# Where the low half of a split weight is subtracted: VectorE, or a summing transfer issued by GpSimd

## The chip, the cores and the metric

The kernel runs on one core of one Trainium2 chip. The metric is device time in microseconds (us) of one execution. TensorE is called PE, VectorE DVE, ScalarE ACT, GpSimd POOL and SyncE SP, as in the profile.

## The reference

```python
def _attn_ref(q, k, v):                      # q, k, v: (8, 8, 576, 64)
    scores = (1.0 / np.sqrt(D)) * np.matmul(q, k.transpose(0, 1, 3, 2))
    mask = (rel >= 0) & (rel < 64)           # rel: query position less key position
    scores = np.where(mask, scores, -1000000000.0)
    attn = np.exp(scores - np.max(scores, axis=-1, keepdims=True))
    attn = attn / (np.sum(attn, axis=-1, keepdims=True) + 1e-09)
    return np.matmul(attn, v)

def _moe_ref(x, w_in, w_out):                # x: (4608, 512), w_in: (512, 2048), w_out: (2048, 512)
    h = x @ w_in
    g = h * np.tanh(np.log1p(np.exp(h)))     # Mish
    return g @ w_out
```

Attention in a sliding window of 64 keys is followed by a feed-forward layer with Mish. The inputs and the output are float32.

## The kernel before, in words

**Split numbers.** Float32 products are made of three products of rounded numbers (type fp32r). Every operand is split into a high part, which is its value rounded to fp32r, and a low part, which is the value less the high part; then high times high, high times low and low times high are summed. For the activations these are `xh`, `xl`, `gh`, `gl`; for the weights `wi_h`, `wi_l`, `wo_h`, `wo_l`, which stay in SBUF for the whole run.

**Weight pieces.** The weights arrive in 32 pieces of 128 x 512 elements, 16 of `w_in` and 16 of `w_out`, in alternation. They are called here by kind and number in the order of work: in0, in1, out0, in2, out1, in3, out2, in4 and so on. The weights come as 64-bit words (512 KB for a piece), and DVE makes float32 of them: `w_abs` takes the sign off (on DVE, or on ACT as an Abs activation while the attention of the start runs), and `w_bits` has four steps, called [0] to [3] here, of which [0] and [1] are a TENSOR_SCALAR and [2] and [3] a SCALAR_TENSOR_TENSOR. The finished float32 piece stands in a tile `wa` (`af` in the code). Then `w_round` lets ACT copy it into the fp32r tile of the high part (a CAST in the profile), and `w_rest` lets DVE subtract the high part from `wa` into the low part.

**Buffers.** `wa` shares the pool tag "t" (4 buffers) with `t`, the float32 Mish result, and with the output tile `o`. So an instruction that begins a new tile of this tag waits until the last reader of an older one is done.

**Stages.** The tokens are worked in 12 chunks of 384. In the **prelude** the attention of chunks 0 and 1 runs in eight units (four pairs of heads for each chunk, u = 0 to 7, and a closing round u = 8). A unit is: score products on PE; mask and row maximum on DVE; six exponentials on ACT; sum, reciprocal on DVE; the normalising product on POOL (`pr<-pr,sm`); transposes on PE into `t_ps`; two copies `pT<-t_ps`, one on ACT and one on DVE; value products on PE (`o_ps`); and the split of the result into `xh` (ACT) and `xl` (DVE). A generator, `stream`, deals the weight work into the units: `OPS` says how many of its steps a unit takes (three or four), and `w_round` stands at the end of each unit.

After it come the **steps**, one for each chunk and each 128 of the 2048 hidden columns: twelve products `h_ps`, two Mish activations on ACT (`t` and `gh`, from the same bank), the residue `gl` = `t` - `gh`, and nine products `acc`. There are two `h_ps` banks, so the products of a step need the Mish activations of two steps earlier. Chunks 0 and 1 go through the steps together, in the order (0,0), (0,1), (0,2), (1,0), (0,3), (1,1) and so on, written (chunk, column block). In these first 32 steps the function `weights` works about one piece for each step, and `gl` is made on DVE. After that POOL makes `gl`, and the attention of later chunks is spread between the steps.

**What sets the order.** In the prelude and the first 32 steps the instructions of DVE, ACT, POOL and SP stand in the order in which the code issues them (`InTurn`); later ones are ordered by a scheduler. Each engine works its instructions strictly one after the other. Between the last unit and the steps, POOL builds the masks of the later chunks (`build_masks`), which takes memsets, affine selects and copies.

Of the kernel before, what the change touches and what calls it, by code (L numbers as in the profile page):

```python
# [10 lines left out]
F32 = mybir.dt.float32  # L11
# [4 lines left out]
ALU = mybir.AluOpType  # L16
# [13 lines left out]
def tile_window_attn_mish_ffn(  # L30
# [11 lines left out]
    NPAIR, _, NT = qT.shape  # L42
    NF, _, NC_, _ = w_in.shape
# [73 lines left out]
    vec, act, pool, load = (InTurn(e) for e in (nc.vector, nc.scalar, nc.gpsimd, nc.sync))  # L117
# [263 lines left out]
    loaded, worked, rounded = [], [], []  # L381

    def w_load():
        if pieces:
            fn, f = pieces.pop(0)
            loaded.append(fn(f))

    def w_abs(by_act):

        if not loaded:  # L390
            return
        st, wh, wl, first = loaded.pop(0)
        words = st.bitcast(U32).rearrange("p (n two) -> p n two", two=2)
        lo, hi = words[:, :, 0], words[:, :, 1]
        a = mp.tile([P, WP], U32, name="wa", tag="t", bufs=4)
        af = a.bitcast(F32)
        if by_act:
            act.activation(af, hi.bitcast(F32), AF.Abs)
        else:
            vec.tensor_scalar(a, hi, 0x7FFFFFFF, None, ALU.bitwise_and)  # L400
        worked.append([lo, hi, a, af, wh, wl, 0])

    def w_bits(parts=range(4)):

        for part in parts:
            at = next((i for i, w in enumerate(worked) if w[-1] == part), None)
            if at is None:
                continue
            lo, hi, a, af, wh, wl, _ = worked[at]
            worked[at][-1] += 1  # L410
            if part == 0:
                vec.tensor_scalar(af, af, BIG, TINY, ALU.min, ALU.max)
            elif part == 1:
                vec.tensor_scalar(a, a, 3, 0x3FFFFFFF, ALU.logical_shift_left, ALU.bitwise_and)
            elif part == 2:
                vec.scalar_tensor_tensor(a, hi, 0xC0000000, a, ALU.bitwise_and, ALU.bitwise_or)
            else:
                vec.scalar_tensor_tensor(a, lo, 29, a, ALU.logical_shift_right, ALU.bitwise_or)
                rounded.append([af, wh, wl, False])
                worked.pop(at)  # L420

    def w_round():
        for r in rounded:
            if not r[3]:
                act.copy(r[1], r[0])
                r[3] = True

    def w_rest():
        while rounded and rounded[0][3]:
            af, wh, wl, _ = rounded.pop(0)  # L430
            vec.tensor_tensor(wl, af, wh.bitcast(F32), ALU.subtract)


    slow = []
# [190 lines left out]
    def stream():  # L625

        while True:
            w_bits([0])
            yield
            if rounded and rounded[0][3]:  # L630
                w_rest()
                yield
            w_bits([1])
            yield
            w_bits([2])
            w_abs(True)
            yield
            w_bits([3])
            w_load()
            yield  # L640
# [3 lines left out]
    early = []  # L644
    products_of(0)
    ops = stream()
    for u in range(U + 1):
        now = u < U
# [40 lines left out]
        if u == U:  # L689
            rest_high(u - 1)  # L690
            rest_low(u - 1)
        w_round()
        if now:
            a.te_transpose(p, [at_bank("t_ps") if u == U - 1 else acc_bank(h, "t_ps") if u == U - 2 else h_bank("t_ps") for h in range(2)])

    w_rest()
    while not worked or worked[0][-1] != 2 or len(worked) > 1:
        if not worked:
            w_abs(False)
        w_bits([worked[0][-1]])  # L700
        if not worked:
            w_load()
            w_round()
# [16 lines left out]
    def weights():  # L720
        residue()
        w_abs(False)
        w_bits([2])
        w_rest()
        w_bits([0, 3, 1])
        w_load()
# [26 lines left out]
    for n, (c, f) in enumerate(steps):  # L753
# [14 lines left out]
        if held[0]:  # L768
            w_round()
            if n not in SCORES:  # L770
                weights()
            if last - 3 <= n < last - 1:
                third.load(n - last + 3, "v")
            if last < n < last + NPAIR:
                third.values(n - last - 1, h_bank)
# [47 lines left out]
```

## Time and profile before

| | |
|---|---|
| median of 3 runs (lowest to highest) | 920.12 us (919.44 to 920.77) |
| the profiled execution | 919.01 us, of which the span is 917.2 us |
| granted TensorE clock, mean | 0.999 |
| PE busy | 893.5 us, 97% of the span |
| ACT busy | 388.3 us, 42% |
| DVE busy | 280.1 us, 31% |
| POOL busy | 184.1 us, 20% |

The rows of a timeline give start, length, engine, line of the code, operation, output and inputs, and in brackets how long the engine sat idle before and what ended that. Line 111 is the helper through which most instructions of DVE, ACT, POOL and SP are issued, and line 120 the one for matmuls, so the tile names tell the groups apart. A group's row gives the busy time, the mean length of one in ns, and the idle time ahead of it.

### The profile page before, as it was taken

What the parts mean: (1) busy time and instruction counts of PE and PEld (TensorE: products, weight loads), DVE (VectorE), ACT (ScalarE), POOL (GpSimd) and SP (SyncE); (2) the same over time, 40 slices, a digit from 0 to 9 for tenths busy, and PEclk for the clock granted to TensorE, in tenths of its full rate; (3) what the DMA queues carried; (4) which work ended last, traced back from release to release, by engine and by line L of the source; (5) the groups of instructions that cost most, each with busy time, mean ns of one, the idle gap of its engine ahead of it and who ended that gap; (6) DMA issues with size and microseconds to landing.
All of it is one profiled execution on the core that took longest, in us unless ns stands there. A gap on an engine that the chain in (4) does not pass through costs nothing.

```text
span 917.2 us, 18683 instructions
## 1 busy us (share of the span) xinstructions
PE 893.5 (97%) x7344; PEld 801.2 (87%) x7344; DVE 280.1 (31%) x1054; ACT 388.3 (42%) x1108; POOL 184.1 (20%) x202
## 2 busy tenths in 40 slices
PE   4799999999999999999999999999999999999998
PEld 3588889888898998998999999999999898899996
DVE  5998898213213032032130230321312303200000
ACT  5843654346545255244342442543524515422211
POOL 3310000021222221222222122122222222122221
PEclk9999999999999999999999999999999999999999
DMA  7834352422322033123121321321213203210000
GB/s 242 267 121 148 123 190 82 136 79 79 102 91 78 21 111 96 27 87 100 46 80 55 95 76 60 91 81 62 84 33 115 78 23 100 69 27 1 35 0 35
DMA packets 84951, 78.56 MB, mean 86 GB/s; under 512 B 11136, under 2 KB 76160, under 8 KB 84864
## 3 DMA queue, kind: packets, MB, share of 16 engines
q1 hardware_dynamic: 79680, 67.94, 24.3%
q10 hardware_dynamic: 5184, 9.44, 2.8%
q8 instruction: 58, 0.95, 0.4%
q14 instruction: 29, 0.24, 0.1%
HBM read 56.10 MB, written 9.44 MB: 71 GB/s over the span
## 4 chain that ended last, share of the span: by engine, by line
PE 94%; ACT 2%; SPq 1%; DVE 1%; DMA 1%; issue 0%; ACTq 0%
PE acc L120 44%; PE h_ps L120 43%; PE o_ps L120 4%; PE s_ps L120 3%; SPq L111 1%; ACT pr L111 1%; DMA k_t<-kT 1%; DVE pT L111 0%; ACT xh L111 0%; DMA pT<-tr 0%; DVE pr L111 0%; DVE wa L111 0%; DVE sm L111 0%; ACT L111 0%; DVE wo_l L111 0%
## 5 line engine op out<-in xcount | busy, mean ns | idle before, releaser
L111 ACT ACTIVATE t<-h_ps 128x384 f32<-128x384 f32 x192 | 94.5, 492 | 449.3 <-PE h_ps L120 427.0
L111 POOL TENSOR_TENSOR gl<-t,gh 128x384 fp32r<-128x384 f32 x160 | 162.1, 1013 | 588.8 <-ACT gh L111 587.3
L120 PE MATMUL h_ps<-xh,wi_h 128*128 128x384 f32 x768 | 259.2, 338 | 0.0
L120 PE MATMUL h_ps<-xh,wi_l 128*128 128x384 f32 x768 | 259.2, 337 | 0.0
L120 PE MATMUL h_ps<-xl,wi_h 128*128 128x384 f32 x768 | 257.9, 336 | 0.0
L120 PE MATMUL acc<-wo_h,gh 128*128 128x512 f32 x576 | 228.8, 397 | 0.0
L120 PE MATMUL acc<-wo_l,gh 128*128 128x512 f32 x576 | 226.8, 394 | 0.0
L120 PE MATMUL acc<-wo_h,gl 128*128 128x512 f32 x576 | 223.5, 389 | 0.0
L120 PEld LDWEIGHTS h_ps<-xh,wi_h 128*128 128x128 f32 x768 | 144.2, 188 | 8.6
L120 PEld LDWEIGHTS h_ps<-xl,wi_h 128*128 128x128 f32 x768 | 144.2, 188 | 7.1
L120 PEld LDWEIGHTS h_ps<-xh,wi_l 128*128 128x128 f32 x768 | 144.0, 188 | 0.0
L120 PEld LDWEIGHTS acc<-wo_h,gl 128*128 128x128 f32 x576 | 108.1, 188 | 24.3
L120 PEld LDWEIGHTS acc<-wo_h,gh 128*128 128x128 f32 x576 | 108.0, 187 | 20.4
L120 PEld LDWEIGHTS acc<-wo_l,gh 128*128 128x128 f32 x576 | 108.3, 188 | 14.8
L111 ACT ACTIVATE pr<-pr,mx 128x96 f32<-128x96 f32 (+1 forms) x288 | 105.2, 367 | 9.0 <-DVE mx L111 8.8
L283 DVE CAST xh<-o_ps 128x256 fp32r<-128x256 f32 x16 | 6.8, 425 | 332.9 <-PE o_ps L120 332.9
L111 ACT ACTIVATE gh<-h_ps 128x384 fp32r<-128x384 f32 x192 | 93.2, 485 | 0.0
L111 DVE CUSTOM_DVE_ANT_0 pr<-s_ps,mask 128x96 f32<-128x96 f32 (+1 forms) x288 | 55.2, 258 | 32.4 <-PE s_ps L120 27.3
L363 DVE COPY o<-acc 128x512 f32<-128x512 f32 x12 | 8.3, 691 | 171.6 <-PE acc L120 171.6
L111 ACT ACT_TABLE_LOAD x45 | 57.7, 1283 | 5.5 <-DVE mx L111 4.8
L111 ACT ACTIVATION_READ_ACCUMULATOR pr<-pr,mx 128x1 f32 x288 | 53.9, 187 | 0.0
L120 PEld LDWEIGHTS o_ps<-pT,v_t 128*64 128x64 f32 x1152 | 38.1, 139 | 16.6 <-ACT pT L111 6.5
(45 smaller groups left out, 463.7 us busy)
## 6 DMA issues: line engine op xcount, KB each, us to landing
v_t<-vN SPq DMA_DIRECT2D x48, 384.0 KB, 4.3
pT<-tr SPq DMA_DIRECT2D x480, 24.0 KB, 1.8
k_t<-kT SPq DMA_DIRECT2D x47, 224.0 KB, 5.0
out<-o ACTq DMA_DIRECT2D x36, 256.0 KB, 2.5
q_t<-qT SPq DMA_DIRECT2D x47, 192.0 KB, 4.5
st<-w_in SPq DMA_DIRECT2D x16, 512.0 KB, 3.6
st<-w_out SPq DMA_DIRECT2D x16, 512.0 KB, 3.5
q_t<-qT SPq DMA_DIRECT2D x3, 64.0 KB, 2.1
```

The costliest lines, as they stand in the source:

```text
L111: i = call(*args, **kw)
L120: order.append(nc.tensor.matmul(*args, **kw).ins)
L283: nc.vector.tensor_copy(xh[:, :cut], o_ps[0])
L363: nc.vector.tensor_copy(o, acc[t])
```

## The change

`w_rest` does nothing any more. `w_round` takes each finished piece, copies it on ACT into the high part as before, lets ACT write the negated value (rounded to fp32r, so the negated high part) into the low part, and lets POOL issue a transfer that adds `wa` to the low part in place. The step of `stream` that was the subtraction is gone from the generator, so with the same `OPS` its other steps move up.

```diff
     def w_round():
-        for r in rounded:
-            if not r[3]:
-                act.copy(r[1], r[0])
-                r[3] = True
+        while rounded:
+            af, wh, wl, _ = rounded.pop(0)
+            act.copy(wh, af)
+            act.mul(wl, af, -1.0)
+            pool.dma_start(wl, af, accum_op=ALU.add)
 
     def w_rest():
-        while rounded and rounded[0][3]:
-            af, wh, wl, _ = rounded.pop(0)
-            vec.tensor_tensor(wl, af, wh.bitcast(F32), ALU.subtract)
+        pass
...
         while True:
             w_bits([0])
             yield
-            if rounded and rounded[0][3]:
-                w_rest()
-                yield
             w_bits([1])
```

Three places of the new order follow. In brackets stands what a row waits for: an engine's name, `DMAHW` for a transfer that SP or ACT issues, and `DMASW` for one that POOL issues. Eight `DMASW` semaphores are used in turn, so DMASW0 to DMASW7 are the transfers of in0, in1, out0, in2, out1, in3, out2 and in4, and the next pieces begin with DMASW0 again.

ACT at the end of the prelude, before, from the first Mish to the third:

```order
L111 ACT_TABLE_LOAD
L111 ACTIVATE t<-h_ps 128x384 [waits Activation_49]
L111 ACTIVATE gh<-h_ps 128x384
L111 CAST wo_h<-wa 128x512 [waits DVE_49]
L111 CAST xh_577<-o_ps 128x384 [waits PE_49]
L111 COPY pT_107<-t_ps 128x3x4x32 [waits PE_49,Activation_49]
L111 ACTIVATE t<-h_ps 128x384 [waits DVE_49,Activation_49]
L111 ACTIVATE gh<-h_ps 128x384
L111 CAST xh_577<-o_ps 128x384 [waits PE_49]
L111 CAST wi_h<-wa 128x512
L111 CAST wo_h<-wa 128x512 [waits DVE_49]
L111 ACTIVATE t<-h_ps 128x384 [waits PE_49,Activation_49]
```

ACT at the same place now, from the first Mish to the second (the Abs of a weight piece is the row `wa<-st`):

```order
L111 ACT_TABLE_LOAD
L111 ACTIVATE t<-h_ps 128x384 [waits DMASW3_49]
L111 ACTIVATE gh<-h_ps 128x384
L111 CAST wi_h<-wa 128x512 [waits DVE_49]
L111 ACTIVATE wi_l<-wa 128x512
L111 CAST xh_587<-o_ps 128x384 [waits PE_49]
L111 ACT_TABLE_LOAD [waits DMAHW6_49,DMASW4_49]
L111 ACTIVATE wa<-st 128x512 [waits Activation_49]
L111 COPY pT_107<-t_ps 128x3x4x32 [waits PE_49]
L111 ACT_TABLE_LOAD [waits DMASW5_49]
L111 ACTIVATE t<-h_ps 128x384 [waits Activation_49]
L111 ACTIVATE gh<-h_ps 128x384
```

The piece cast behind the first Mish is in3 and no longer out1, an Abs has come between the two Mish steps with a table load on each side, and the second Mish stands behind a wait for the transfer of in3.

ACT in the rows that follow now, up to the fourth Mish:

```order
L111 CAST xh_587<-o_ps 128x384 [waits PE_49]
L111 CAST wo_h<-wa 128x512 [waits DVE_49]
L111 ACTIVATE wo_l<-wa 128x512
L111 CAST wi_h<-wa 128x512 [waits DVE_49]
L111 ACTIVATE wi_l<-wa 128x512
L111 ACTIVATE t<-h_ps 128x384 [waits DMASW6_49,PE_49,Activation_49]
L111 ACTIVATE gh<-h_ps 128x384
L111 CAST wo_h<-wa 128x512 [waits DVE_49]
L111 ACTIVATE wo_l<-wa 128x512
L111 ACTIVATE t<-h_ps 128x384 [waits DMASW7_49,PE_49,Activation_49]
```

The third Mish waits for the transfer of out2 and the fourth for that of in4, where the third waited before for PE and ACT alone.

POOL between the last normalising product and the steps, now (before, the masks follow the product at once and no transfer stands here):

```order
L111 DMA wi_l<-wa 128x512 [waits Activation_49]
L111 DMA wo_l<-wa 128x512 [waits DVE_49,Activation_49]
L111 MEMSET mask 128x128
L111 AFFINE_SELECT mask<-mask 32x96 [waits Pool_49]
L111 AFFINE_SELECT mask<-mask 32x96 x3
L111 AFFINE_SELECT mask<-mask 32x96 [waits Pool_49] x4
L111 COPY mask_83<-mask 128x128 [waits Pool_49]
L111 MEMSET mask_83 32x64 [waits Pool_49]
L111 MEMSET mask_83 32x32
L111 COPY mask_84<-mask 128x128 [waits Pool_49]
...
L111 DMA wi_l<-wa 128x512 [waits DVE_49,Activation_49]
```

The transfers of in3 and out2 stand ahead of the masks and that of in4 behind them.

## The prediction

> **What bounds the kernel now.** I read the page of the profile first, for the busy shares and the chain that ended last:
>
> ```profile
> span 917.2 us, 18683 instructions
> PE 893.5 (97%) x7344; PEld 801.2 (87%) x7344; DVE 280.1 (31%) x1054; ACT 388.3 (42%) x1108; POOL 184.1 (20%) x202
> PE 94%; ACT 2%; SPq 1%; DVE 1%; DMA 1%; issue 0%; ACTq 0%
> ```
>
> PE carries the run; it is idle for 917.2 - 893.5 = 23.7 us in all. The windows by stage say where (columns: length, then busy time and count of PE, PE's weight loads, DVE, ACT and POOL, then clock, share of the DMA engines, GB/s):
>
> ```profile
> 0.00:23.00 23.00, 11.43 (x152) 8.52 (x154) 12.41 (x63) 12.26 (x46) 7.93 (x20) 1.00 0.75 242
> 23.00:46.00 23.00, 16.83 (x273) 13.55 (x268) 21.64 (x94) 20.63 (x79) 8.31 (x8) 1.00 0.87 265
> 46.00:69.00 23.00, 21.98 (x135) 20.02 (x134) 21.39 (x46) 10.08 (x21) 3.90 (x14) 1.00 0.38 124
> 69.00:92.00 23.00, 23.00 (x160) 20.60 (x159) 18.56 (x50) 7.50 (x17) 0.00 (x0) 1.00 0.44 147
> ```
>
> Nearly all of it, 11.6 + 6.2 + 1.0 us, lies ahead of 69 us. From there PE is full although DVE, which makes the weights, is busy 18.6 of 23 us. So a lighter DVE buys nothing behind the prelude; the change can gain only what it takes off the prelude, and it loses whatever it makes PE wait. The timeline of PE shows where the prelude ends:
>
> ```profile
> 47.59 0.82 PE L301 MATMUL t_ps<-ident,pr 128*128 128x128 f32 x6
> 48.70 0.33 PE L120 MATMUL o_ps<-pT,v_t 128*64 128x64 f32 x2 [0.30 <-ACT pT L111]
> 49.75 0.91 PE L120 MATMUL o_ps<-pT,v_t 128*64 128x64 f32 x22 [0.72 <-DVE pT L111]
> 50.59 0.44 PE L120 MATMUL h_ps<-xh,wi_h 128*128 128x384 f32 x1
> ...
> 54.84 0.33 PE L120 MATMUL h_ps<-xh,wi_h 128*128 128x384 f32 x1
> ...
> 63.17 0.33 PE L120 MATMUL h_ps<-xh,wi_h 128*128 128x384 f32 x1
> ```
>
> The last wait is at 49.75, for DVE's copy of the last unit's `pT`. The products of step (0,2) start at 50.59, of (1,0) at 54.84 and of (1,1) at 63.17; two steps take 63.17 - 54.84 = 8.33 us, without a gap.
>
> **The change part by part: what goes and what comes.** The groups by form give the prices:
>
> ```profile
> L111 DVE TENSOR_TENSOR wo_l<-wa,wo_h 128x512 fp32r<-128x512 f32 x16 | 11.0, 688 | 0.2 <-ACT wo_h L111 0.2
> L111 DVE TENSOR_TENSOR wi_l<-wa,wi_h 128x512 fp32r<-128x512 f32 x16 | 11.0, 686 | 0.1
> L111 ACT CAST wi_h<-wa 128x512 fp32r<-128x512 f32 x16 | 9.9, 621 | 10.4 <-DVE wa L111 10.4
> L111 ACT ACT_TABLE_LOAD x45 | 57.7, 1283 | 5.5 <-DVE mx L111 4.8
> L111 POOL TENSOR_TENSOR gl<-t,gh 128x384 fp32r<-128x384 f32 x160 | 162.1, 1013 | 588.8 <-ACT gh L111 587.3
> L111 DVE TENSOR_SCALAR wa<-wa 128x512 uint32<-128x512 uint32 x32 | 13.5, 422 | 0.1
> ```
>
> DVE loses 32 subtractions, 22.0 us. ACT gains 32 negations; the nearest row is the cast over the same tile, 0.62 us (0.51 from start to start, as the rows below show). ACT also gains two table loads of 1.28 us at the end of the prelude, because the stream, one step shorter, now brings an Abs between the first two Mish steps. POOL gains 32 issues and the DMA engines 32 transfers of 128 x 512 float32, 256 KB each. From 69 us on ACT has 15 idle us in 23 and PE needs none of this soon, so there I cost the negations and transfers at nothing.
>
> **The units of the prelude.** The waits ahead of an exponential show ACT's room:
>
> ```profile
> 31.11 0.40 ACT L111 ACTIVATE pr<-pr,mx 128x128 f32<-128x128 f32 x1 [0.42 <-DVE mx L111]
> ...
> 40.22 0.40 ACT L111 ACTIVATE pr<-pr,mx 128x128 f32<-128x128 f32 x1 [0.82 <-DVE mx L111]
> ```
>
> A unit is a loop: exponentials, then on DVE the sum, one weight step, reciprocal, the copy of `pT` and the next masks. The subtractions of DVE stood mostly beside the exponentials, off this loop; the negations fill the 0.42 to 0.82 us that ACT waits. Walking the new order through with the row lengths of before, units 3 and 6 start up to 0.5 us earlier or later, and the eighth unit's exponentials start at 40.2, as before. I cost the units at nothing, with 1 us either way.
>
> **The end of the prelude: +1.05 us.** Timelines of ACT and of DVE:
>
> ```profile
> 44.16 1.28 ACT L111 ACT_TABLE_LOAD   x1
> 45.46 0.49 ACT L111 ACTIVATE t<-h_ps 128x384 f32<-128x384 f32 x1
> 45.85 0.48 ACT L111 ACTIVATE gh<-h_ps 128x384 fp32r<-128x384 f32 x1
> 46.22 0.62 ACT L111 CAST wo_h<-wa 128x512 fp32r<-128x512 f32 x1
> 46.73 0.49 ACT L111 CAST xh<-o_ps 128x384 fp32r<-128x384 f32 x1
> 48.17 0.48 ACT L111 COPY pT<-t_ps 128x384 f32<-128x384 f32 x1 [0.95 <-PE t_ps L301]
> 48.92 0.49 ACT L111 ACTIVATE t<-h_ps 128x384 f32<-128x384 f32 x1 [0.27 <-DVE wo_l L111]
> ```
>
> ```profile
> 47.25 0.56 DVE L111 TENSOR_TENSOR xl<-o_ps,xh 128x384 fp32r<-128x384 f32 x1 [1.13 <-ACT xh L111]
> 47.73 0.43 DVE L111 TENSOR_SCALAR wa<-wa 128x512 f32<-128x512 f32 x1
> 48.08 0.74 DVE L111 TENSOR_TENSOR wo_l<-wa,wo_h 128x512 fp32r<-128x512 f32 x1
> ...
> 49.15 0.54 DVE L111 COPY pT<-t_ps 128x384 f32<-128x384 f32 x1
> ```
>
> Now, from the cast at 46.22: negation 46.73 to 47.30, `xh` at 47.24, table load 47.6 to 48.9, Abs to 49.5, ACT's `pT` to 49.95 (before 48.65). DVE stands behind that Abs with step [0], at 49.5, then step [1] at 49.85 and its `pT` copy at 50.2, where before it came at 49.15. So the value products end their wait at 50.8 for 49.75, and every later product of PE is 1.05 us late.
>
> **The wait chain in the first steps: +2.3 us.** Let L be the time from the end of a negation until its transfer is reported done. A Mish begins a new tile of tag "t" and now waits for transfers. Second Mish: in3's transfer is done at 47.3 + L, a table load follows, so it starts at 48.6 + L. With the spacing of the rows above (Mish to `gh` 0.39, `gh` to the next 0.37, 0.37 for `xh`, 0.51 for a cast), the negation of out2 ends at 50.8 + L. Third Mish: out2's transfer, 50.8 + 2L. On POOL the issue of out2 (taken as 1.0 us by the nearest row, 1013 ns for a product over such a tile; between 0.4 and 1.5 it matters little) is followed by the masks:
>
> ```profile
> 45.52 0.21 POOL L111 MEMSET mask<- 128x128 f32 x1
> ...
> 49.80 0.52 POOL L111 COPY mask<-mask 128x128 f32<-128x128 f32 x1
> ```
>
> They take 50.32 - 45.52 = 4.8 us, and nobody waited for that before. Now in4's transfer queues behind them: issue at 50.8 + L + 1.0 + 4.8 = 56.6 + L, done at 56.6 + 2L, and the fourth Mish with its `gh` has left its bank 0.9 later, at 57.5 + 2L. The products of (1,1) need that bank at 63.17 + 1.05 = 64.2. PE therefore waits 2L - 6.7 us if that is above nothing. The third Mish asks for less (2L + 51.7 against 60.05), and later Mish steps catch up as long as 1.9 us of ACT work and L fit into the 8.33 us of two steps.
>
> L is not in this trace: no transfer here is issued by POOL or sums. The nearest rows, issue to landing:
>
> ```profile
> v_t<-vN SPq DMA_DIRECT2D x48, 384.0 KB, 4.3
> pT<-tr SPq DMA_DIRECT2D x480, 24.0 KB, 1.8
> k_t<-kT SPq DMA_DIRECT2D x47, 224.0 KB, 5.0
> ```
>
> The low end is the small transfer from SBUF to SBUF plus 256 KB at 320 GB/s (0.98 of the engines moved 314 GB/s in a row quoted below), 1.8 + 0.8 = 2.6 us; the high end is the 224 KB row with 1.0 for the issue and as much again for reading the destination, 7.0. I take 4.5, by the two rows nearest in size, 4.3 and 5.0. The wait is then 2 x 4.5 - 6.7 = 2.3 us. By the Trainium skill (DMA: Bandwidth & Descriptors, section "Anatomy of one DMA — SWDGE (gpsimd) path") a transfer issued by GpSimd takes about 2.0 us and bytes over 436e3, an estimate of 2.6 us here; no row here shows it, and by it the sum would end at +1.05.
>
> **The sum.** 919.01 + 1.05 + 2.3 = 922.4 us for a profiled execution. That one lay 1.1 us under the median, so the median goes from 920.1 to 923.5.
>
> **The rivals.** *Short transfers*: with L up to 3.35 the chain hides, and only the 1.05 is left, 921.2 us. For it speaks the 1.8 us row; against it that POOL must make the issue and the transfer reads two streams. The estimate from the page is this case. Chance 0.20.
>
> *Long transfers*: with L from 6 to 7 the sum is 1.05 + 5.3 to 7.3, 926.5 to 928.5 us, and over 6.4 (8.33 - 1.9) each further pair of steps loses too. A mechanism would be that DVE's short TENSOR_SCALAR rows, 0.42 us for 512 columns where the subtraction takes 0.69, hold off POOL's issue: up to 0.84 for two in a row. By the Trainium skill (SBUF — State Buffer, section "SBUF: two separate sides") a VectorE operation of a two-port mode keeps GpSimd from writing descriptors; no run here shows it. Chance 0.17.
>
> *Crowded DMA in the prelude*: the units run with nearly full DMA engines:
>
> ```profile
> 25.50:30.00 4.50, 2.93 (x54) 2.25 (x54) 4.10 (x21) 3.84 (x16) 1.47 (x1) 1.00 0.93 299
> ...
> 34.00:38.50 4.50, 2.93 (x54) 2.25 (x54) 4.12 (x20) 4.14 (x17) 1.47 (x1) 1.00 0.98 314
> ```
>
> Six more transfers at 0.8 to 1.6 us and one more weight load of 512 KB (1.6) make 6.4 to 11.2 us on top of 0.87 x 23 = 20 in 23 us, so 3.4 to 8.2 too many. Queries, keys and values are loaded a unit or two ahead, which covers about 4 us; beyond that units stretch. At 2.5 us on top of the sum it gives 926. Chance 0.10.
>
> *A shorter prelude, faster than before*: if DVE, busy 21.6 of 23 us, does set the pace of the units, the five subtractions that stood ahead of 49 us (the last of them is the row at 48.08) give back up to 5 x 0.69 = 3.4 us. It turns into a gain from the point where more than the 1.05 of the table loads reaches PE, with a short L beside it; at its full price 920.1 - 3.4 + 1.05 = 917.7 us. Against it: DVE waits for the exponentials in each unit, and ACT, which makes them, gets more to do. Chance 0.08.
>
> **How the numbers follow.** The forecast, L between 3.7 and 6, has 0.45 and gives 921.9 to 926.5 by itself. The measurement can tell about 0.2%, 1.84 us, from no change. Faster is the last rival, 0.08; within 0.2% are the short transfers, 0.20; slower is the rest, 0.72. The range leaves out the faster case and the far end of the long transfers: from 920.6 (short transfers with half a us of gain in the units) to 929.0.
>
> **What would show it.** Right: 47 table loads for 45; ACT's last `pT` copy near 49.5 and DVE's near 50.2; the second Mish at 53 and the fourth at 65 to 66, each waiting for a transfer; a gap of PE of some 2 us ahead of the products of (1,1); PE full from 75 us on. Wrong: a first `h_ps` product far from 40.9, which is the units; gaps that go on behind 80 us, which is L over 6.4; no gap after 51 us, which is a short L.

## The result, and the profile after

| | before | after |
|---|---|---|
| median (lowest to highest) | 920.08 us (919.44 to 920.77, 4 runs) | 929.62 us (927.66 to 931.55, 4 runs) |
| profiled execution, its span | 919.01, 917.2 us | 929.78, 927.9 us |
| mean granted clock | 0.999 | 0.994 |

The ratio is 1.0103, with a 95% interval of 1.0081 to 1.0126: 9.5 us slower. The direction was forecast, the size was not; 929.62 lies above the range's upper end of 929.0.

The page after, the span, the engines and the queue of the transfers that POOL issues (packets, MB, share of 16 engines):

```profile
span 927.9 us, 18783 instructions
PE 897.1 (97%) x7344; PEld 804.5 (87%) x7344; DVE 263.2 (28%) x1021; ACT 407.1 (44%) x1143; POOL 214.1 (23%) x234
...
q0 software_dynamic: 4608, 8.39, 5.5%
```

The windows by stage, with the same limits as before:

```profile
0.00:23.00 23.00, 10.01 (x134) 7.39 (x134) 11.08 (x56) 12.18 (x45) 8.05 (x20) 1.00 0.77 244
23.00:46.00 23.00, 16.56 (x258) 13.36 (x257) 19.49 (x95) 21.66 (x82) 10.59 (x9) 0.93 1.02 300
46.00:69.00 23.00, 19.67 (x129) 17.52 (x129) 14.45 (x30) 12.69 (x22) 12.04 (x20) 0.93 0.60 166
69.00:92.00 23.00, 20.66 (x138) 18.54 (x139) 15.28 (x43) 11.57 (x24) 5.30 (x6) 0.93 0.82 193
```

Three things stand in these rows. PE is idle longer in each of the four stages (25.1 us in all against 18.8). From 23 to 92 us the granted clock is 0.93 where it was 1.00. The share of the DMA engines has risen to 1.02, 0.60 and 0.82 from 0.87, 0.38 and 0.44 (it is the sum of the packets' times over the time of 16 engines, so it can pass 1).

The timeline of PE after, from the last unit to the products of (1,1). The products of step (0,2) start at 54.03, of (1,0) at 59.85, of (1,1) at 71.34:

```profile
52.17 0.33 PE L120 MATMUL o_ps<-pT,v_t 128*64 128x64 f32 x2 [1.19 <-ACT pT L111]
53.19 0.91 PE L120 MATMUL o_ps<-pT,v_t 128*64 128x64 f32 x22 [0.69 <-DVE pT L111]
54.03 0.44 PE L120 MATMUL h_ps<-xh,wi_h 128*128 128x384 f32 x1
...
54.90 0.52 PE L120 MATMUL h_ps<-xh,wi_h 128*128 128x384 f32 x1
...
59.85 0.33 PE L120 MATMUL h_ps<-xh,wi_h 128*128 128x384 f32 x1
...
71.34 0.65 PE L120 MATMUL h_ps<-xh,wi_h 128*128 128x384 f32 x1 [3.00 <-ACT gh L111]
...
72.43 0.53 PE L120 MATMUL h_ps<-xh,wi_h 128*128 128x384 f32 x1
```

Against before they are late by 3.44 us (54.03 - 50.59), 5.01 (59.85 - 54.84) and 8.17 (71.34 - 63.17). Between the first two, no wait is added: the rows last 0.52 us where they lasted 0.33, so PE ran at about half speed. At (1,1) PE waits 3.00 us for the fourth Mish, and behind that the rows last 0.53 again. The granted clock was 0.50 from 54.35 to 57.76 us and from 71.42 to 74.83: a half-speed stretch lasts 3.4 us and costs about half of that, here 1.57 and 1.66 us. A third one, from 33.87 to 37.28 us, lies in the units. These three make the 0.93 of the three stages.

The timelines of ACT and POOL after show why the fourth Mish is late:

```profile
49.79 1.28 ACT L111 ACT_TABLE_LOAD   x1
51.09 0.66 ACT L111 ACTIVATE wa<-st 128x512 f32<-128x512 f32 x1
51.65 0.47 ACT L111 COPY pT<-t_ps 128x384 f32<-128x384 f32 x1
53.29 1.28 ACT L111 ACT_TABLE_LOAD   x1 [1.17 <-DMA wi_l<-wa]
...
61.19 0.49 ACT L111 ACTIVATE t<-h_ps 128x384 f32<-128x384 f32 x1 [1.62 <-DMA wo_l<-wa]
...
70.42 0.49 ACT L111 ACTIVATE t<-h_ps 128x384 f32<-128x384 f32 x1 [7.32 <-DMA wi_l<-wa]
```

```profile
57.17 0.86 POOL L111 DMA_DIRECT2D wo_l<-wa  x1 [6.58 <-ACT wo_l L111]
57.89 0.34 POOL L111 MEMSET mask<- 128x128 f32 x1
58.31 5.41 POOL L111 TENSOR_SCALAR_AFFINE_SELECT mask<-mask 32x96 f32<-32x96 f32 x8
...
65.51 0.47 POOL L111 MEMSET mask<- 32x64 f32 x2
66.00 0.86 POOL L111 DMA_DIRECT2D wi_l<-wa  x1
66.56 1.18 POOL L111 DMA_DIRECT2D wo_l<-wa  x1
```

The Abs with its two table loads, the waits of the second, third and fourth Mish for in3's, out2's and in4's transfers, and in4's issue behind the masks all stand where the prediction put them. The masks take 8.1 us (57.89 to 65.98) where the prediction took 4.8.

### The profile page after: what moved, and what is told of

Its sections match the earlier page's. It is cut to its first block, busy times and chain, and to the rows that moved or that the text cites. A ratio compares the mean times of both kernels' runs of the same rounds, so it can differ in the third digit from the quotient of the medians.

```text
span 927.9 us, 18783 instructions
## 1 busy us (share of the span) xinstructions
PE 897.1 (97%) x7344; PEld 804.5 (87%) x7344; DVE 263.2 (28%) x1021; ACT 407.1 (44%) x1143; POOL 214.1 (23%) x234
## 3 DMA queue, kind: packets, MB, share of 16 engines
q0 software_dynamic: 4608, 8.39, 5.5%
## 4 chain that ended last, share of the span: by engine, by line
PE 92%; ACT 3%; issue 1%; DMA 1%; SPq 1%; POOL 1%; DVE 0%; POOLq 0%; ACTq 0%
PE h_ps L120 43%; PE acc L120 43%; PE o_ps L120 4%; PE s_ps L120 3%; ACT pr L111 1%; DMA k_t<-kT 1%; SPq L111 1%; POOL mask L111 0%; DMA wi_l<-wa 0%; ACT pT L111 0%; ACT xh L111 0%; ACT wi_h L111 0%; ACT wi_l L111 0%; DVE wa L111 0%; ACT L111 0%
```

## The experiments

The runs were made in five lots; each lot timed the kernel before beside it (919.2 to 919.8 us). The table gathers what the sections below use. Starts of products are from the one profiled execution; "third scores" are the third unit's score products, whose start is set by the first loads.

| kernel | median us | third scores | (0,0) | (0,2) | (1,1) | span |
|---|---|---|---|---|---|---|
| before | 920.08 | 15.74 | 40.88 | 50.59 | 63.17 | 917.2 |
| after | 929.62 | 17.28 | 42.91 | 54.03 | 71.34 | 927.9 |
| after_again | 929.50 | 16.23 | 41.89 | 52.99 | 70.46 | 927.6 |
| after_third | 928.92 | 16.38 | 42.05 | 53.16 | 67.42 | 927.1 |
| prelude_only | 924.02 | 15.76 | 42.34 | 54.85 | 67.43 | 921.9 |
| steps_only | 924.28 | 15.82 | 40.92 | 50.62 | 64.06 | 921.9 |
| no_idle | 921.20 | 15.77 | 41.15 | 52.36 | 64.95 | 919.3 |
| neg_add | 920.48 | 16.66 | 42.06 | 52.28 | 64.89 | 918.7 |
| prelude_idle | 920.22 | 16.21 | 41.37 | 50.95 | 63.54 | 918.4 |
| idle_step | 930.05 | 16.72 | 41.81 | 51.51 | 71.17 | 927.1 |
| masks_parts | 927.86 | 16.91 | 43.81 | 55.64 | 69.80 | 925.4 |
| idle_masks | 924.27 | 15.61 | 41.04 | 50.66 | 64.52 | 922.5 |
| pool_sub | 921.95 | 15.49 | 41.09 | 50.53 | 63.13 | 918.6 |
| plain_copy | 925.82 | 15.77 | 40.72 | 51.82 | 66.95 | 923.3 |

My theory on seeing the profile after was that of the prediction with larger sizes: masks in POOL's queue, then a Mish that waits, then half speed. The rivals were the prelude (crowded DMA engines, later loads) and ScalarE's added work.

### What recurs, and which half loses what

Twice the changed kernel was run unedited:

> The changed kernel once more, unedited, to see which parts of its trace recur. If the late start of the third score products (17.28 us against 15.74) comes from the change: 17.2 us again. If it is a spread of the first loads: anywhere from 15.6 to 17.3 us, with the end moved by as much. The gap of some 3 us ahead of the products of (1,1) and the half clock behind it should be there again, and the masks should take 8 us again, if they are causes and not accidents. Time 928 to 932 us.

> The changed kernel once more, unedited, beside the kernel with the filled gap: a gap of 3 to 4.7 us ahead of (1,1) and rows of 0.52 us behind it, 928 to 932 us. Without a half clock behind such a gap the theory of the gap falls.

The time recurs, 929.50 and 928.92. The start does not: third scores at 16.23 and 16.38, and 15.5 to 17.3 over all kernels, those without a transfer among them. So most of the 1.54 us by which the profile after starts late are a spread of the first loads. The gap ahead of (1,1) recurs in kind and not in size, 4.73 and 1.51 us; where it is small, PE loses the same later (2.1 us of idle time and a clock of 0.96 between 92 and 138 us).

The three profiles of the changed kernel show where it loses its time. The table gives how much later than before PE gets through each stretch, in us:

| stretch | after | after_again | after_third |
|---|---|---|---|
| up to the third scores (first loads) | 1.54 | 0.49 | 0.64 |
| third scores to (0,2): units, end of the prelude | 1.90 | 1.91 | 1.93 |
| (0,2) to (1,0): half speed alone | 1.57 | 0.00 | 0.00 |
| (1,0) to (1,1): the wait for the fourth Mish | 3.16 | 4.89 | 1.68 |
| (1,1) to (0,4): half speed | 1.66 | 1.98 | 0.08 |
| the rest | 0.9 | 1.1 | 5.5 |
| span | 10.7 | 10.4 | 9.8 |

The sizes of the gap follow from the masks. From the first MEMSET to the issue of in4's transfer they took 8.1, 8.2 and 5.8 us, and from there to the fourth Mish 4.4, 4.5 and 3.7 us passed. After_third's gap is 3.2 us smaller than after_again's, by 2.4 of masks and 0.8 of transfer; after's is 1.7 smaller, because half speed brought PE to it 1.57 us later.

Next, one half of the change at a time:

```diff
+    by_pool = [True]
     def w_round():
...
+        if by_pool[0]:
+            while rounded:
+                af, wh, wl, _ = rounded.pop(0)
+                act.mul(wl, af, -1.0)
+                pool.dma_start(wl, af, accum_op=ALU.add)
...
     build_masks(pool, TQ)
...
     third = atts[2]
+    by_pool[0] = False
```

That is prelude_only; in steps_only `False` stands first and `True` below.

> The negation and the transfer only for the pieces of the prelude; in the steps behind it VectorE subtracts as before, so no transfer is queued behind the masks but what the prelude left. If nearly all of the loss is the wait behind the masks and what follows it: 921 to 923 us, PE without a gap ahead of (1,1). If crowded DMA engines and the table loads of the prelude carry it: 925 us and more, the first product of h_ps at 42 to 43 us as in the changed kernel.

> VectorE subtracts in the prelude as before; only in the steps behind it are negation and transfer used. The prelude should then be that of the kernel before (first product of h_ps at 40.9 us, products of (0,2) at 50.6, give or take the 0.8 us of the first loads). If the masks in the queue carry the loss: a gap of PE of 3 us or more ahead of a product of the steps (1,0) to (1,2), half clock behind it, 924 to 926 us. If the prelude carries it: 920 to 921 us.

Measured: 924.02 us (ratio 1.0052, 1.0033 to 1.0071) and 924.28 (1.0053, 1.0034 to 1.0072). Each half loses about the same, 4.4 and 4.7 us, and the sum of 9.1 is nearly the whole change's 9.5. The traces do not add up that way, though: net of the first loads, prelude_only's profile loses 4.2 us up to (0,2) where the three of the whole change lose 1.9, and those lose 7.3 to 8.0 us behind it. My theory held for neither: the prelude alone loses 4.4 us with no transfer behind the masks, and the steps alone lose 4.7 though there the masks stand ahead of every transfer.

### The prelude: the shorter stream and the transfers

> The kernel before with ScalarE's negation into the low part, to which VectorE then adds the piece: ScalarE's new work alone, with the old cadence, no transfer. By the prediction the 32 negations of 0.62 us cost nothing: 920 us, at most 921, with 45 table loads. If ScalarE's new work stretches the units of the prelude: the first product of h_ps at 41.5 us or later, 921 to 923 us.

The diff against before: the negation is written to the low part, and VectorE adds the piece (`act.mul(r[2], r[0], -1.0)` in `w_round`; in `w_rest` `ALU.add` on `wl` for `ALU.subtract` of `wh`). 920.48 us, 1.0008 (0.9998 to 1.0018): ScalarE's 32 negations cost nothing that can be told.

> The kernel before with VectorE's subtraction, only without the step of the weight stream that it had to itself: no negation, no transfer by GpSimd, but the loads of the weights in the changed kernel's order and its two extra table loads. If the shorter stream is what stretches the prelude (weight loads ahead of query, key and value loads): products of (0,2) at 52.5 to 54.5 us, 922 to 923.5 us. If it costs what the prediction gave it: (0,2) at 51.7, 921 us. If the transfers crowd the prelude and the order of the loads does not matter: 920 us.

```diff
             if rounded and rounded[0][3]:
                 w_rest()
-                yield
             w_bits([1])
```

921.20 us, 1.0016 (1.0007 to 1.0025), products of (0,2) 1.77 us late. The prediction had 1.05 for it, between (0,1) and (0,2). Only 0.41 us lies there in this profile and 1.08 between (0,0) and (0,1), so the run prices the shorter stream as a whole and doesn't part its table loads from its earlier weight loads.

> The kernel with negation and transfer only in the prelude, now also with the idle step in the stream, so that the loads of the weights stand where they stood before. If the prelude's loss is the two together, the transfers on DMA engines that the earlier loads fill: 919.5 to 921 us, the products of (0,2) at 50.6 us, give or take the first loads. If the transfers alone carry it: 922.5 us and more, (0,2) at 53 us or later.

```diff
                 pool.dma_start(wl, af, accum_op=ALU.add)
+                due.append(wl)
...
-            if rounded and rounded[0][3]:
-                w_rest()
+            if due:
+                due.clear()
                 yield
```

920.22 us, 1.0006 (0.9997 to 1.0016): the transfers alone cost nothing. So the shorter stream costs 1.5 to 2 us, the transfers nothing, and both together 4.4. The loads that SP issues, in the kernel before and in the kernel with the prelude's half of the change:

```profile
27.76 0.38 SPq L111 DMA_DIRECT2D v_t<-vN  x1
...
31.26 0.38 SPq L111 DMA_DIRECT2D st<-w_in  x1
...
31.86 0.38 SPq L111 DMA_DIRECT2D v_t<-vN  x1
```

```profile
26.36 0.54 SPq L111 DMA_DIRECT2D st<-w_in  x1
...
27.86 0.38 SPq L111 DMA_DIRECT2D v_t<-vN  x1
...
32.04 1.53 SPq L111 DMA_DIRECT2D st<-w_out  x1
...
33.67 0.39 SPq L111 DMA_DIRECT2D v_t<-vN  x1
```

A weight load (512 KB) that stood at 31.26 now stands at 26.36, ahead of a unit's values. From 23 to 46 us the share of the DMA engines is 0.87 before, 0.88 in no_idle, 0.99 in prelude_idle and 1.06 in prelude_only. In prelude_only PE waits for values. The window from 30 to 34 us and the wait, in the kernel with the prelude's half:

```profile
30.00:34.00 4.00, 3.88 (x74) 3.08 (x66) 3.78 (x19) 4.00 (x14) 2.28 (x2) 0.78 1.09 317
```

```profile
36.36 0.92 PE L120 MATMUL o_ps<-pT,v_t 128*64 128x64 f32 x24 [2.10 <-DMA v_t<-vN]
```

In the kernel before, the same window has a share of 0.77, and PE waits for no values in the units:

```profile
30.00:34.00 4.00, 2.93 (x54) 2.25 (x54) 3.86 (x20) 3.58 (x16) 1.47 (x1) 1.00 0.77 218
```

With the prelude's half and the idle step the share in this window is 0.90 (1.07 in the one before it), and the wait for values is gone again:

```profile
30.00:34.00 4.00, 2.84 (x62) 2.15 (x55) 3.64 (x19) 4.00 (x17) 2.28 (x2) 1.00 0.90 258
```

Two limits to this. Of prelude_only's 4.2 us, 1.4 lie in the units and 2.8 between (0,0) and (0,2), where the clock was 0.50 from 42.02 to 45.43 us: part of what the two cost together is half speed. And the changed kernel itself, with shares of 1.01 to 1.05 from 23 to 46 us, loses 0.5 us in the units in each of its three profiles and waits for values 0.35 us in one and not at all in two. Full engines alone don't decide; what does is open.

> The kernel before with the 32 subtractions on GpSimd in place of VectorE, in the same steps of the stream; no negation, no transfer. It measures what VectorE's relief is worth by itself. If VectorE sets the pace of the units: 917 to 918.5 us, the first product of h_ps ahead of 40 us. If its subtractions stood beside other waits: 919.5 to 920.5 us. If GpSimd and VectorE hinder each other: 921 us and more, the masks later and longer.

The diff is `pool` for `vec` in `w_rest`. 921.95 us, 1.0026 (1.0015 to 1.0037): slower. The first product of `h_ps` stands at 41.09, so relieving DVE shortened no unit. But the run doesn't measure the relief cleanly, since POOL's work slowed DVE's (last section).

### The steps: masks, or any transfer

> The changed kernel with one idle step of the weight stream where the subtraction stood, so that the Mish steps fall where they fell before and the two extra table loads go. Theory of the prediction (the loads cost 1.05 us at the end of the prelude, the masks in the queue of GpSimd stay): 928.5 us, 45 table loads, the gap of PE ahead of the products of (1,1) still some 3 us with its half-clock stretch. Rival (the order of the stream matters little, the loads lay beside other waits): 929.5 us, the milestones of the prelude unchanged. Rival (the stretch of half clock at 54 to 57.5 us hangs on the late end of the prelude): that stretch goes too, 926.5 to 927 us.

> The changed kernel with GpSimd's masks built one part in each step, where they stood all at once between out2's and in4's transfers. Theory A (the 8.1 us of masks ahead of in4's transfer make the fourth Mish late): the gap of 3.15 us ahead of the products of (1,1) goes, and with it the 1.65 us of half clock behind it, so 929.6 - 4.8 = 924.8 us. Rival B (two transfers of 4.4 us in a row are long enough by themselves): 928.5 us or more, the fourth Mish still waiting for its transfer. Rival C (the gap goes but the half clock does not hang on it): 926.5 us.

> Both edits, the idle step and the masks in parts. If their shares add up: 1.05 us under the kernel with the masks in parts alone, 923.7 us by theory A with the theory of the prediction; 922 us if the half-clock stretch at 54 to 57.5 us goes as well; what is then left over the kernel before, 2 to 3.5 us, lies ahead of the first product of h_ps. If the masks in parts gain nothing: as the kernel with the idle step.

The first edit is the idle step as above. The second deals the masks out:

```diff
     def build_masks(engine, tq):
...
+            yield
...
-    build_masks(pool, TQ)
+    late = build_masks(pool, TQ)
...
             w_round()
+            next(late, None)
```

Measured: 930.05 (927.92 to 933.36), 927.86 (924.15 to 929.96) and 924.27 us (923.85 to 925.97). The idle step alone mends the prelude, (0,2) at 51.51, and gains nothing, because now the masks stand ahead of a piece of `w_out` that PE itself waits for:

```profile
68.44 0.80 PE L120 MATMUL acc<-wo_l,gh 128*128 128x512 f32 x1 [5.57 <-DMA wo_l<-wa]
...
71.17 0.52 PE L120 MATMUL h_ps<-xh,wi_h 128*128 128x384 f32 x1
```

With the masks in parts the gap ahead of (1,1) and the half speed behind it are gone, as theory A said (the products of (0,3), at 65.63, and of (1,1), at 69.80, follow at 4.17 us). Two things did that: the eight selects still stand ahead of in4's transfer, but its issue comes 4.8 us behind out2's and not 8.8, and PE comes 1.6 us later than in the profile after. The time fell by only 1.8 us and not 4.8, since the prelude was 1.6 us slower in this profile than after's, and its spread is wide. Both edits together take off 5.4 us. What is left, 4.5 us over before, is as much as steps_only loses, though in waits of 1.0 us and less and without half speed.

Across these profiles, a late prelude and waits in the steps replace each other in part. Masks_parts comes to (1,0) 6.6 us late and has no wait from 60 to 140 us; idle_masks comes 0.1 us late and loses some 5 us behind it. So shares that are measured one at a time need not add up.

So I turned to the transfer. ACT in steps_only:

```profile
62.62 0.49 ACT L111 ACTIVATE t<-h_ps 128x384 f32<-128x384 f32 x1 [4.89 <-DMA wo_l<-wa]
...
88.65 0.49 ACT L111 ACTIVATE t<-h_ps 128x384 f32<-128x384 f32 x1 [6.13 <-DMA wi_l<-wa]
...
95.87 0.49 ACT L111 ACTIVATE t<-h_ps 128x384 f32<-128x384 f32 x1 [2.69 <-DMA wo_l<-wa]
```

```profile
96.80 0.70 PE L120 MATMUL s_ps<-k_t,q_t 64*32 64x96 f32 x26 [1.78 <-ACT gh L111]
```

These Mish steps wait for a transfer, and behind the last of them PE waits 1.78 us and then runs at half speed (clock 0.84 from 92 to 100 us). Was it that a Mish takes a buffer which a transfer still reads? Two edits took that away:

> The changed kernel with the rounded pieces' source tiles and the Mish tiles in two rings of two buffers in the first steps, where they shared one ring of four: a Mish then waits for no transfer, but the masks still stand ahead of in4's transfer. If the ring is what carries the wait from the transfer to PE: the fourth Mish starts without a wait, no gap ahead of (1,1), no half clock behind it, 924.8 us. Rival (the wait only moves: the next load into a source tile, or the weight itself, is then late): 927 to 929.6 us, with a gap of PE at a later product that names a weight tile or a load.

```diff
-        t = mp.tile([P, CH], F32, name="t", tag="t", bufs=4)
+        t = mp.tile([P, CH], F32, name="t", tag="t" if held[0] else next(tags), bufs=2)
...
-        a = mp.tile([P, WP], U32, name="wa", tag="t", bufs=4)
+        a = mp.tile([P, WP], U32, name="wa", tag="wa" if stepping[0] else next(tags), bufs=2)
```

1002.83 us. Two buffers for `wa` starve the weights: between 60 and 300 us DVE waits 49.3 + 37.7 us for transfers to let go of a piece. Later I gave the Mish one buffer of its own and left three for `wa` and `o`:

```diff
-        t = mp.tile([P, CH], F32, name="t", tag="t", bufs=4)
+        t = mp.tile([P, CH], F32, name="t", tag="t", bufs=1)
...
-        a = mp.tile([P, WP], U32, name="wa", tag="t", bufs=4)
+        a = mp.tile([P, WP], U32, name="wa", tag="wa", bufs=3)
```

> Control: the kernel before with its shared ring of four buffers split, one buffer for the Mish tile t, three for the pieces wa and the stores o. It tells what the split itself costs. If one t is enough (its product gl follows within 1.1 us): 920 us. If Mish then waits for gl: 922 us or more, and the two kernels below have to be read against this one.

> The changed kernel with the split ring: no Mish waits for a transfer any more, all else as it was, the masks too. If the wait of the Mish for transfers is what carries the loss of the steps: the control plus the prelude's loss of 3.5 to 4.4 us, so 924 us with a control of 920, and no gap of PE ahead of (1,1) put down to ScalarE. If the weights themselves are late: PE waits for wi_l or wo_l in its place, 927 us or more.

> The kernel with transfers only in the steps, with the split ring. If the Mish's wait for transfers made its loss of 4.7 us: within 1 us of the control, PE without a gap from 60 to 140 us. If the lateness of the weights or the DMA traffic made it: 3 us or more above the control.

919.33, 928.63 and 924.84 us. The split is free (1.0001, 0.9992 to 1.0010) and it mends nothing, so the theory of the Mish's wait fell. The wait moved to DVE. Timelines of DVE, ACT and PE in ring_steps:

```profile
79.41 0.43 DVE L111 TENSOR_SCALAR wa<-st 128x512 uint32<-128x512 uint32 x1 [3.07 <-DMA wo_l<-wa]
```

```profile
81.41 0.62 ACT L111 CAST wo_h<-wa 128x512 fp32r<-128x512 f32 x1 [3.93 <-DVE wa L111]
81.93 0.63 ACT L111 ACTIVATE wo_l<-wa 128x512 fp32r<-128x512 f32 x1
82.46 0.47 ACT L111 ACTIVATE t<-h_ps 128x384 f32<-128x384 f32 x1
82.83 0.48 ACT L111 ACTIVATE gh<-h_ps 128x384 fp32r<-128x384 f32 x1
```

```profile
83.37 0.70 PE L120 MATMUL s_ps<-k_t,q_t 64*32 64x96 f32 x26 [1.20 <-ACT gh L111]
84.00 0.69 PE L120 MATMUL acc<-wo_h,gh 128*128 128x512 f32 x1
84.49 0.63 PE L120 MATMUL acc<-wo_l,gh 128*128 128x512 f32 x1
```

DVE can't begin the next piece until a transfer has read its buffer; ACT waits for that piece with a Mish queued behind it; PE waits for the Mish and then runs at half speed. A piece's buffer that is held until its transfer lands hands the wait to whoever needs one next. That this is the cause in the steps agrees with both layouts, with neg_add (the same negations, no transfer, no loss) and with the next run. It isn't shown by a run that takes the loss away: a layout with enough buffers for both was not tried.

### The transfer itself

> The changed kernel with transfers that copy the piece over the low part instead of adding to it; left out is the sum, so the low part holds the piece and not the residue. If the sum is what makes the transfer long (two streams read): the transfer's median from issue to landing falls from 4.1 to about 3 us, the gap ahead of (1,1) from 3.0 to 4.7 to 1 to 3 us, 926 to 928 us. If the length is the issue by GpSimd and the path: 4 us and 929 to 930 us as with the sum.

The diff: `accum_op=ALU.add` is gone. 925.82 us (1.0067, 1.0053 to 1.0081), 3.8 under the kernel after, or 3.0 with each set against the kernel before in its own lot. Its queue, and a transfer's time from issue to landing (min, median, max) for `wi_l` after and for `wi_l` here:

```profile
q0 software_dynamic: 2560, 8.39, 2.4%
```

```profile
DMA to landing us min/median/max: 3.3/4.1/7.2
```

```profile
DMA to landing us min/median/max: 2.2/2.8/5.9
```

The same 8.39 MB take 2.4% of 16 engines for 5.5%: a summing transfer costs 1.6 us of all sixteen (0.055 x 927.9 / 32), a copying one 0.7 (0.024 x 923.3 / 32). It lands 1.3 us later at the median, and either takes 6 to 7 at worst. Here the prelude is what the prediction walked through: (0,2) at 51.82, 1.23 us late, and a gap of 2.39 us ahead of (1,1).

> The changed kernel with each transfer as two of 128 KB. If bytes make the length: each half lands in some 2.5 us, the second half some 3.5 to 4 us after the first issue, 929 us as before. If a fixed part makes it: each half takes 3.5 us or more, the second lands 0.9 us later than the whole one did, every wait for a transfer grows by that, 930.5 to 932 us.

The diff: two transfers of 256 columns each. 941.06 us (1.0253, 1.0223 to 1.0284), 11.4 slower than after and far over both expectations. A half takes 4.4 us (`wi_l`) or 4.0 (`wo_l`) at the median, about as long as a whole one, and twice as many of them queue. At best it lands in 2.6 us for 3.3, so part of the median is the queue.

### The half clock

> The changed kernel with 17 products of 0.17 us more, into a bank that nobody reads, ahead of the products of (1,1): they fill 3 us of the gap in which PE waits for the fourth Mish. If it is the gap that makes the half clock behind it: the rows of (1,1) last 0.33 us for 0.52 and its products 2.1 us for 3.8, so the end comes 1.65 us earlier, 928 us. If the half clock does not hang on the gap: rows of 0.52 us as before and 929.6 us or more.

```diff
     def first_half(n):
         c, f = steps[n]
+        if n == 5:
+            fill, (xh, _) = at_bank("fill"), atts[0].x
+            with in_order():
+                for _ in range(17):
+                    pe(fill, wi_h[:, 0, 0, :], xh[:, 0, :], start=True, stop=True)
```

929.66 us (928.77 to 930.64): 3 us of added products cost nothing on the whole, and rows of (1,1) lasted 0.33 us. But in its profile the prelude was later, (0,2) at 55.32, the fourth Mish stood at 68.70, and the added products began at 69.46 without a gap to fill. So it settles nothing on the half clock.

The traces taken together say more. Behind every gap of PE of 1.76 us and more from 60 us on, in the kernels that the table lists, halves and ring_after, there is a stretch of half speed that begins in the gap or at most 1.8 us behind it: 1.76 (halves), 1.78 (steps_only), 2.14 (after_third), 2.36 (ring_after), 2.39 (plain_copy), 3.00 (after), 4.73 (after_again), 5.57 (idle_step). Behind gaps of 1.1 to 1.7 us it sometimes is (1.20, ring_steps) and sometimes not (1.51, after_third). The kernel before has no gap over 1.05 us behind 20 us and no such stretch. But ahead of 60 us gaps of 1.9 to 2.0 us (at 42.06, 41.05 and 41.20 in the three profiles of the changed kernel) have none behind them, and the stretch at 54.35 in after has only gaps of 1.19 and 0.69 us ahead of it.

The idle time within a fixed window fits better than the single gap. In each of the 20 profiles the granted clock is 1.00 or 0.50, and up to 900 us it changes only at whole multiples of 3.41 us, counted from its first change to 1.00. After, the window before the stretch and the stretch (columns as above; PE is busy for 1.53 us in the first):

```profile
50.94:54.35 3.41, 1.53 (x27) 1.29 (x27) 1.81 (x5) 2.23 (x4) 0.00 (x0) 1.00 0.92 234
54.35:57.76 3.41, 3.41 (x12) 3.41 (x11) 2.28 (x6) 2.51 (x6) 0.59 (x1) 0.50 0.00 1
```

Over the 20 profiles, 22 windows at full clock had PE busy for under 1.6 us, and all 22 were followed by half clock. Of 75 with 1.6 to 2.25 us, 15 were; of 5015 busier ones, none. So the 1.20 us in ring_steps and the 1.51 in after_third lie in the range where both happen. The Trainium skill (TensorE: Matmul & The Clock Gate, section "Part 1: The HAM clock gate (the "warmup" mystery)") says that PE falls to half rate after an idle window of some 3.4 us and needs as long to come back. The 3.4 us of the slow stretches agree with the second; with the first these traces do not, since a window in which PE was idle for 1.20 of 3.41 us sufficed (ring_steps).

## Why the prediction was right in direction and short in size

*PE is the bound and DVE's relief buys nothing behind the prelude*: right. DVE's busy time fell by 17 us and the time did not. ("Nearly all" of PE's idle time ahead of 69 us was four fifths, 18.8 of 23.7 us.)

*Negations cost nothing*: right (neg_add, 1.0008).

*The end of the prelude, +1.05 us*: right as a mechanism. The Abs and its two table loads stand as walked through. In the three profiles of the changed kernel (0,0) to (0,2) takes 1.4 us longer, 0.9 of it at the place that was named.

*The units, nothing with 1 us either way*: 0.5 us in those three profiles, which is within it. It failed in prelude_only, where the units took 1.4 us longer with a wait of 2.10 us for values, and half speed at (0,0) came on top. The rival of the crowded prelude described this wait, at a chance of 0.10 and a price of 2.5 us; it did not say that the transfers alone are harmless, and the changed kernel's own three profiles show almost none of this wait.

*The wait chain, 2L - 6.7 = +2.3 us with L = 4.5*: the chain is the one in the trace, and L was near: in4's issue and the fourth Mish are 4.4, 4.5 and 3.7 us apart in the three profiles, in3's from the end of the negation to the table load 3.9. L came from loads of a similar size that SP issues, which neither sum nor stay in SBUF, so there was luck in it; a copying transfer on the same path landed in 2.8 us at the median and a summing one in 4.1. The masks were mis-sized, 5.8 to 8.2 us for 4.8. PE waited 3.0, 4.7 and 1.5 us. That the first is near the forecast is luck too: the fourth Mish came some 5 us later than forecast and PE some 4.

*What no term held, and the step that failed*: the sum charged each wait of PE with its own length and took PE to run at full speed behind it. In the profile after PE ran at half clock from 54.35 to 57.76 and from 71.42 to 74.83 us, which cost 1.57 and 1.66 us, 3.2 of the 10.7 by which its span grew; in after_again the stretch behind the gap cost 2.0. Terms of 1.05 and 2.3 became 1.9 and 3.2 (the first with the units' 0.5), 1.54 us more are a late start that the reruns do not show to that extent, and 0.9 lie behind: 1.54 + 1.90 + 1.57 + 3.16 + 1.66 + 0.9 = 10.7.

*From 69 us on, negations and transfers at nothing*: right up to 180 us in the profiles after and after_again, and wrong in after_third, which loses 4 us near 100 us, and in steps_only, which loses 3.8 us between 86 and 101 us with no masks in the way. "Catch up as long as 1.9 us of ACT work and L fit into the 8.33 us" took L as 4.5 always. In the trace after, a transfer lands in 3.3 to 7.2 us, with weight loads beside it, and a piece's buffer is held that long.

The rivals *short transfers* (L up to 3.35) and *faster* fell: the median to landing was 4.1 us, and no run shows a unit that became shorter because DVE had less to do.

No version beat the kernel before: of what was tried, the nearest are prelude_idle and neg_add, which can't be told from it.

## What to carry to other kernels

Before work is moved from an engine that is not the bound to a transfer, ask how long the transfer holds its source, and who needs that buffer next: the wait comes out at whichever engine claims it first, and splitting the ring only moves it. Two changes of which one cost nothing alone (more transfers) and the other 1.5 to 2 us (a shorter stream, with loads issued earlier) cost 4.4 us together in prelude_only, so measure them together. Where new gaps leave PE busy for less than half of a 3.41 us window, add about 1.65 us for the half speed behind it.

## What the runs showed of the hardware

A summing transfer from SBUF to SBUF used the DMA engines 2.3 times as long as a copying one of the same 256 KB (1.6 us of all sixteen against 0.7), and one of 128 KB took about as long from issue to landing as one of 256 KB (4.0 to 4.4 us at the median for 4.1), with twice as many in the queue.

Eight affine selects of the masks took 5.41 us after, for 3.15 before. It was one of them, the first behind a transfer's issue:

```profile
58.31 2.74 POOL L111 TENSOR_SCALAR_AFFINE_SELECT mask<-mask 32x96 f32<-32x96 f32 x1
```

After_again has it too. After_third does not (3.72 us for the eight), and in ring_after they take 2.95 us behind an issue; kernels without a transfer range from 2.99 (neg_add) to 4.07 (pool_sub). What stretches them is open.

Subtractions on POOL slowed DVE. In pool_sub DVE's busy time was 286 us, 6 more than before, though it had 22 us of work less. The groups of its SCALAR_TENSOR_TENSOR, before and there:

```profile
L111 DVE SCALAR_TENSOR_TENSOR wa<-st,wa 128x512 uint32<-128x512 uint32 x64 | 44.8, 700 | 0.0
```

```profile
L111 DVE SCALAR_TENSOR_TENSOR wa<-st,wa 128x512 uint32<-128x512 uint32 x64 | 59.1, 924 | 0.1
...
L111 POOL TENSOR_TENSOR wi_l<-wa,wi_h 128x512 fp32r<-128x512 f32 x16 | 28.5, 1783 | 33.8 <-ACT wi_h L111 33.8
```

The mean goes from 700 to 924 ns. POOL's subtraction takes 1783 ns for `wi_l` and 1440 for `wo_l`, where the prediction's nearest row, 1013 for three quarters of the columns, would have said about 1350.
